# Loading the first two groups' records on SyncE behind later scatters, and one more routing step per chunk

## Chip, cores and metric

The kernel runs on one NeuronCore of a Trainium2 chip. The metric is the device time of one execution in microseconds; lower is better. Engines are written as in the profile: PE (TensorE), DVE (VectorE), ACT (ScalarE), POOL (GpSimd) and SP (SyncE, which here only issues DMAs).

## What is computed

A pooled attention (8 batches, 8 heads, 576 queries, head size 64, keys and values averaged over 8 positions to 72) is followed by a mixture of 8 experts, of which each of the 4608 tokens takes two, chosen by noisy logits. Cut to what matters:

```
k_p = k.reshape(B, H, Sp, pool, D).mean(axis=3)
v_p = v.reshape(B, H, Sp, pool, D).mean(axis=3)
attn = softmax(scale * q @ k_p^T);  x = attn @ v_p      # x: 4608 x 512
noisy_logits = x @ w_gate + log1p(exp(x @ w_noise)) * noise
top2 = the two largest of 8;  top2_w = softmax over the two
out[mask] += top2_w * (relu(x[mask] @ w1[e]) @ w2[e])   # w1: 512 x 1024, w2: 1024 x 512
```

## The kernel before

**Attention and routing.** The 36 chunks of 128 tokens are worked through in four pairs of batches (pair 0 to 3, nine chunks each). PE transposes queries (qp), multiplies them with pooled keys (s), transposes the exponentials (ep) and multiplies with pooled values (a, with the operand vbd that DVE makes from vr); DVE divides and writes the chunk (xr_b_i, batch b), and SP writes two chunks at a time to x_dram from four buffers. When a pair's logits are complete, its routing (`route`, a generator) runs in steps between the instructions of the next pair's chunks: `advance(n, m)` runs n steps of the oldest routing and then issues up to m items of the queue `scq`. Each chunk calls it with n = STEPS[pr] = 2 at one place (`adv`), and with n = 0 at up to two others (L932). Pair 3 has no next pair: its routing runs during the first stage 1 of the experts.

A routing first picks the top two on DVE and makes a mask mb. Ten small matmuls rk (L606) count the tokens per expert with mb as their operand; DVE then makes positions (pos) and records (rec, four words per token and choice). All of a pair's records are written to rec_dram, sorted by expert, by 18 scatters (L650) on POOL, each 128 rows. Between two indirect DMAs `spaced` puts a spacer, a memset of 128x512 (L501).

**Experts.** Expert 0's tokens are taken in three groups: token tiles 0 to 3, tiles 4 and 5, tiles 6 to 9. `load_recs` loads the records of a group's tiles (raw, L691). `fetch` issues a `gather` (L718) per tile, an indirect DMA on POOL from x_dram into xg. PE transposes xg (L768), stage 1 (L1030) multiplies with w1, ACT and DVE make the two parts of the hidden blocks (hh, hl; eight blocks f), and stage 2 (L1141) multiplies with w2. At the end of a tile DVE makes pv and POOL writes it to slot_dram (L1082). The load and the gathers for tiles 0 to 3 stand on POOL behind pair 1's scatters, since these tiles hold only tokens of pairs 0 and 1; those for tiles 4 and 5 stand behind pair 2's, the gathers for tiles 6 to 9 behind pair 3's. The third load of expert 0's records is issued by SP, the first two by POOL.

Each expert's weights come in eight pieces of 512 KB, loaded by SP into three buffers (wst, L459). ACT casts each piece (L480) and DVE takes the difference (L481). wst_3_1 is an expert's last piece. Each engine, and SP's queue of DMAs, works in the order in which the program issues instructions to it, and a waiting instruction holds those behind it.

Of the kernel before, what the change touches and what calls it, by code (L numbers as in the profile page):

```python
# [19 lines left out]
def kernel(  # L20
# [12 lines left out]
    nc = tc.nc  # L33
# [12 lines left out]
    NP = B // 2  # L46
    NCH = 9
# [81 lines left out]
    QS = 2  # L129
    WU = 16  # L130
    H0 = 80
    RE = 1
    PT = dict(zip(('kT', 'vTp', 'vr'), [{'o': 'one', 's': 's'}[c] for c in 'ooo']))
    EV = 0
    XE = 0
# [4 lines left out]
    STEPS = (2, 2, 2, 2)  # L140
# [350 lines left out]
    scq = []  # L491
    pace = [None]
    tail_ind = [None]
    spacer = [ap_.tile([P, DM], F32, name="spacer")]

    def spaced(make):
        if tail_ind[0] is None:
            tail_ind[0] = make()
        else:
            with tc.issue_after(tail_ind[0].ins):  # L500
                gap = nc.gpsimd.memset(spacer[0], 0.0)  # L501
            with tc.issue_after(gap.ins):
                tail_ind[0] = make()
        return tail_ind[0]

    def route(pr, c0, c1, lg, psum):
        n = c1 - c0
        k_ = [0]
# [140 lines left out]
        def scatter(c, i):  # L649
            s = spaced(lambda: nc.gpsimd.indirect_dma_start(  # L650
                out=rec_dram[:, :],
                out_offset=bass.IndirectOffsetOnAxis(ap=pos[:, i, c:c + 1], axis=0),
                in_=rec[:, c, i, :], in_offset=None))
            tc.declare_no_dep(s.ins, group="rec_scatter", reason="distinct rows")
            if pr >= NP // 2:
                tc.declare_no_dep(s.ins, group="rec_load0", reason="rows of the other half")
            if pr == NP - 1:
                tc.declare_no_dep(s.ins, group="rec_load1", reason="rows of the other pairs")
            tc.add_to_no_dep_group("rec_scatter", s.ins)
            tc.add_manual_dep(s.ins, pace[0].ins.name,  # L660
                              mybir.DependencyInfo(mybir.DependencyClass.Sync, mybir.DependencyReason.DATA),
                              reason="paced")

        for c in range(n):
            for i in range(2):
                scq.append(lambda c=c, i=i: scatter(c, i))
        if pr == NP // 2 - 1:
            scq.append(lambda: load_recs(0, 1, 0, 1, 1))
            scq.append(lambda: fetch(groups[0]))
        if pr == NP - 2:  # L670
            scq.append(lambda: load_recs(0, 1, 1, 2, 2))
            scq.append(lambda: fetch(groups[1]))
        if pr == NP - 1:
            scq.append(lambda: load_recs(0, 1, 2, 4))
            scq.append(lambda: fetch(groups[2]))
# [2 lines left out]
    def load_recs(e0, e1, s0, s1, early=0):  # L678
        ne = e1 - e0
        sect = SECT if e0 else SECT0  # L680
        t0, t1 = sect[s0][0], sect[s1 - 1][0] + sect[s1 - 1][1]
        nt = t1 - t0
        nm = f"{e0}_{t0}"
        V = nc.vector
        raw = rp.tile([P, ne, nt, RW], I32, name=f"raw{nm}")
        if s1 == len(SECT):
            V.memset(raw[64:, :, nt - 1, :], 0)
        src = rec_dram.rearrange("(e r) c -> e (r c)", e=E)
        for ts, n, np_ in sect[s0:s1]:
            o = ts * P * RW  # L690
            ld = (nc.gpsimd if RE >> (0 if early else 1 if e0 == 0 else 2) & 1 else nc.sync).dma_start(raw[:np_, :, ts - t0:ts - t0 + n].rearrange("p e t c -> p e (t c)"),  # L691
                                   src[e0:e1, o:o + np_ * n * RW].rearrange("e (p x) -> p e x", p=np_))
            if early:
                tc.add_to_no_dep_group(f"rec_load{early - 1}", ld.ins)

        for e in range(e0, e1):
            for t in range(t0, t1):
                i = (e - e0, t - t0)
                xi[e, t] = raw[:, i[0], i[1], 0:1]
                tokc[e, t] = raw[:, i[0], i[1], 2:3]  # L700
                mate[e, t] = raw[:, i[0], i[1], 3:4]
                wcol[e, t] = raw.bitcast(F32)[:, i[0], i[1], 1:2]
# [12 lines left out]
    def gather(e, t):  # L715
        xg = wp.tile([P, DM], F32, tag="xg", name=f"xg{e}_{t}", bufs=4)
        if e == 0:
            g = spaced(lambda: nc.gpsimd.indirect_dma_start(  # L718
                out=xg, out_offset=None, in_=x_dram[:XT0 if t < 4 else NTOK, :],
                in_offset=bass.IndirectOffsetOnAxis(ap=xi[e, t], axis=0)))  # L720
            if t < 4:
                tc.declare_no_dep(g.ins, group="xw1", reason="rows of the other half")
                tc.add_to_no_dep_group("xg0", g.ins)
        else:
            nr = 2 if t == 9 else 4
            row = pools[0].tile([P, DM], F32, tag="row", name=f"row{e}_{t}", bufs=4)
            turn_of("pool", lambda: nc.gpsimd.indirect_dma_start(  # L727
                out=row[:32 * nr], out_offset=None, in_=x_dram[:, :],
                in_offset=bass.IndirectOffsetOnAxis(ap=xi[e, t][:32 * nr], axis=0)))
            via = dp.tile([P, DM], F32, tag="via", name=f"via{e}_{t}", bufs=4)  # L730
            for r in range(nr):
                turn_of("sp", lambda: nc.sync.dma_start(
                    via.rearrange("(u j) (r c) -> j r u c", u=4, r=4)[:, r],
                    row[32 * r:32 * r + 32].rearrange("j (u c) -> j u c", u=4)))
            back.append(lambda: turn_of("sp", lambda: nc.sync.dma_start(xg[:, :nr * P], via[:, :nr * P])))
        XG[e, t] = xg
# [7 lines left out]
    def fetch(g):  # L744
        e, t0, nt = g
        for t in range(t0, t0 + nt):
            gather(e, t)
        while back:
            back.pop(0)()
# [44 lines left out]
    def advance(n, m):  # L794
        for _ in range(n):
            while gens:
                try:
                    next(gens[0])
                    break
                except StopIteration:  # L800
                    gens.pop(0)
        for _ in range(min(m, len(scq))):
            scq.pop(0)()
# [38 lines left out]
    for b in range(1, B):  # L842
        c = 9 * (b // 2) + (0 if b % 2 == 0 else 4)
# [44 lines left out]
    for i, (ui, u, jj) in enumerate(chunks):  # L888
        pr, ci = divmod(i, NCH)
        if ci == 0:  # L890
            lgs[pr] = (rp if pr % 2 else ap_).tile([P, NCH, H, 2 * E], F32, tag="lg", name=f"lg{pr}")
        single = u[0] == "R"
        has = ui + 1 < NU
        if single:
            order = OR
        else:
            order = OD[jj]
        eT = None
        quiet = 0 if ci == 0 and pr <= NP // 2 or ci == NCH - 1 and pr < NP // 2 else 1

        def bgs():
            for f in bg.get(i, ()):
                f()

        def adv():
            pace[0] = lastx[0]
            advance(STEPS[pr], 2 * quiet if pr >= NP // 2 else quiet)

        for o in order + ("" if "b" in order else "b") + ("" if "x" in order else "x"):
            if o == "v" and i == 0:  # L910
                drain(pg[0])
            if o == "b":
                bgs()
            elif o == "x":
                adv()
            elif o == "e":
                eT = et(u, jj)
            elif o == "v":
                if due:
                    due.pop()()  # L920
                if ci == NCH - 1 and pr < NP - 1:
                    gens.append(route(pr, 0, NCH, lgs[pr], one))
                elif ci == NCH - 1:
                    rt = route(pr, 0, NCH, lgs[pr], lambda nm: mone(nm))
                    next(rt)
                due.append(lambda u=u, jj=jj, ci=ci, eT=eT, lg=lgs[pr]: av(u, jj, ci, eT, lg))
            elif o in "012":
                if has:
                    qk(units[ui + 1], int(o))
                    if pr and (o == "0" or not single):  # L930
                        pace[0] = lasta[0]
                        advance(0, quiet)  # L932
            elif ui + 2 < NU:
                qtr(units[ui + 2], "qr".index(o))
        if i == 24:
            for _ in range(WS):
                wload()
        if i == 33:
            splits = rows_of(groups[0], one)
        if pr == 3 and ci:  # L940
            with tc.issue_after(lastl[0].ins), tc.issue_after(lasta[0].ins):
                next(first[0], None) if ci < 5 else next(first[1], None)
        if ci == 4 and pr >= HS:
            gens.append(route(pr, 0, 5, lgs[pr], one))
# [34 lines left out]
    for i in range(3):  # L979
        t = mp.tile([P, DM], F32, name=f"pv{i}")  # L980
# [356 lines left out]
```

## Time and profile before

| | |
|---|---|
| median of three runs | 1028.24 us (1027.77 to 1030.14) |
| profiled execution | 1030.06 us, its span 1028.1 us |
| granted clock, mean | 0.983 |
| busy: PE, DVE, ACT, POOL | 994.1, 551.6, 345.0, 415.1 us |
| stage 1 and 2 of the first group | from 185.21 us on |
| stage 1 of the second and third group | from 236.64 and 272.58 us on |

The span is the time from the first to the last instruction. PE is busy for 97% of it; the rest lies in a few places that the timeline shows, most of them before 280 us. A row of a timeline gives start, duration, engine, line, operation, number of instructions and, in brackets, the idle time of the engine before it with what ended that. In a row of a chain of waits stand start, duration, and what the chain runs through there.

### The profile page before, as it was taken

How to read it: one execution, taken by the hardware profiler on the slowest of the kernel's cores; microseconds unless marked ns; L12 is line 12 of the kernel's file. 1: busy time of each engine (PE TensorE's matmuls, PEld its weight loads, DVE VectorE, ACT ScalarE, POOL GpSimd, SP SyncE). 2: the span in 40 equal slices, each digit the busy share in tenths (PEclk: the TensorE clock that was granted, in tenths of full speed). 3: DMA queues.
4: the chain of work that ended last, by engine and by line, in shares of the span. 5: the costliest groups of instructions: out<-in, count | busy, mean ns of one | idle time of the engine just before them, and what ended most of it. 6: DMA issues, size and time to landing. Idle time of an engine off the chain costs nothing.

```text
span 1028.1 us, 16525 instructions
## 1 busy us (share of the span) xinstructions
PE 994.1 (97%) x5832; PEld 890.1 (87%) x5832; DVE 551.6 (54%) x1283; ACT 345.0 (34%) x857; POOL 415.1 (40%) x494
## 2 busy tenths in 40 slices
PE   7999999988899999999999999999999999999996
PEld 6798998867798988898988898989888988898995
DVE  5699988932245454644454446344544455456341
ACT  4687788521113222421232124212321232123120
POOL 4023878968500442155215421552154215422514
PEclk9899999989899999999999999999999999999999
DMA  9986954441707765676267746772677357744623
GB/s 279 341 272 222 321 187 129 142 134 27 222 35 212 205 183 148 192 245 193 76 175 242 216 125 209 243 212 74 184 241 232 114 170 245 244 145 135 210 88 135
DMA packets 137382, 190.36 MB, mean 185 GB/s; under 512 B 29155, under 2 KB 84084, under 8 KB 137274
## 3 DMA queue, kind: packets, MB, share of 16 engines
q1 hardware_dynamic: 111834, 121.84, 39.3%
q0 software_dynamic: 25440, 67.05, 21.2%
q8 instruction: 72, 1.18, 0.5%
q14 instruction: 36, 0.29, 0.1%
HBM read 126.07 MB, written 70.74 MB: 191 GB/s over the span
## 4 chain that ended last, share of the span: by engine, by line
PE 79%; DMA 6%; DVE 5%; POOL 4%; issue 3%; ACT 2%; SPq 1%; POOLq 0%; DVEq 0%; ACTq 0%
PE bank L1030 32%; PE bank L1141 23%; PE bank L1107 10%; PE a L408 5%; PE s L375 3%; PE ep L393 2%; DMA wst<-in_moe_w_dram 2%; PE qp L347 1%; POOL rec_dram L650 1%; DVE w L481 1%; POOL lg L501 1%; DMA v<-in_v_dram 1%; ACT ex L382 1%; POOL out_dram L1086 1%; DMA tab_dram<-tab 1%
## 5 line engine op out<-in xcount | busy, mean ns | idle before, releaser
L1030 PE MATMUL bank<-xh,w 128*128 128x512 f32 (+6 forms) x1536 | 390.6, 338 | 2.1 <-DVE pv L1080 1.5
L1030 PEld LDWEIGHTS bank<-xh,w 128*128 128x128 f32 x1536 | 270.3, 188 | 22.9 <-DVE pv L1080 1.7
L1141 PE MATMUL bank<-w,hh 128*128 128x512 f32 x880 | 273.9, 393 | 0.0
L1030 PE MATMUL bank<-xl,w 128*128 128x512 f32 (+6 forms) x768 | 259.7, 338 | 0.0
L1041 ACT ACTIVATE hh<-bank 128x512 fp32r<-128x512 f32 (+4 forms) x192 | 97.5, 510 | 468.7 <-PE bank L1030 444.6
L1042 DVE SCALAR_TENSOR_TENSOR hl<-bank,hh 128x512 fp32r<-128x512 f32 (+4 forms) x192 | 110.9, 579 | 241.1 <-ACT hh L1041 241.1
L1141 PEld LDWEIGHTS bank<-w,hh 128*128 128x128 f32 x880 | 166.7, 190 | 34.4
L1141 PE MATMUL bank<-w,hl 128*128 128x512 f32 x440 | 172.4, 392 | 0.0
L1030 PEld LDWEIGHTS bank<-xl,w 128*128 128x128 f32 x768 | 144.6, 188 | 10.3
L1082 POOL DMA_DIRECT2D slot_dram<-yt x17 | 9.8, 574 | 266.2 <-DVE yt L1078 218.5
L1078 DVE SCALAR_TENSOR_TENSOR pv<-bank,raw,pv 128x128 f32<-128x128 f32 x196 | 55.5, 343 | 107.0 <-PE bank L1141 58.0
L1107 PE MATMUL bank<-hh,w 128*128 128x240 f32 (+3 forms) x512 | 104.7, 300 | 2.0 <-issue 2.0
L1141 PEld LDWEIGHTS bank<-w,hl 128*128 128x128 f32 x440 | 83.3, 189 | 17.5
L1062 POOL DMA_INDIRECT pv<-slot_dram,raw x70 | 68.6, 980 | 67.9 <-DMA slot_dram<-ys 35.0
L650 POOL DMA_INDIRECT rec_dram<-rec,pos x72 | 81.1, 1127 | 36.7 <-DVE rd L415 24.5
L481 DVE TENSOR_TENSOR w<-wst,w 128x512 fp32r<-128x512 f32 x128 | 82.5, 683 | 10.4 <-ACT w L480 10.4
L1107 PEld LDWEIGHTS bank<-hh,w 128*128 128x128 f32 x512 | 83.9, 192 | 2.2 <-issue 2.2
L727 POOL DMA_INDIRECT row<-x_dram,raw x70 | 71.1, 1016 | 24.7 <-issue 20.0
L480 ACT CAST w<-wst 128x512 fp32r<-128x512 f32 x128 | 72.9, 619 | 22.7 <-DMA wst<-in_moe_w_dram 22.6
L1082 POOL DMA_DIRECT2D slot_dram<-pv x55 | 31.7, 576 | 117.4 <-DVE pv L1078 93.7
L1107 PE MATMUL bank<-hl,w 128*128 128x320 f32 (+3 forms) x256 | 76.5, 299 | 0.0
L382 ACT ACTIVATE ex<-s,mx 128x72 f32<-128x72 f32 x288 | 70.5, 345 | 8.0 <-DVE mx L380 7.8
(167 smaller groups left out, 1073.0 us busy)
## 6 DMA issues: line engine op xcount, KB each, us to landing
wst<-in_moe_w_dram SPq DMA_DIRECT2D x64, 512.0 KB
via<-row SPq DMA_DIRECT2D x266, 64.0 KB
xg<-via SPq DMA_DIRECT2D x63, 256.0 KB
slot_dram<-pv POOLq DMA_DIRECT2D x55, 256.0 KB
k<-in_k_dram SPq DMA_DIRECT2D x7, 1280.0 KB
v<-in_v_dram SPq DMA_DIRECT2D x16, 512.0 KB
x_dram<-xr SPq DMA_DIRECT2D x16, 512.0 KB
q<-in_q_dram SPq DMA_DIRECT2D x7, 1024.0 KB
```

Of the source, the lines that this page charges most:

```text
L382: lasta[0] = nc.scalar.activation(ex[:, jj, EPOS[h] * G:(EPOS[h] + 1) * G], sv[:, i], AF.Exp, bias=mx[:, i:i + 1])
L480: nc.scalar.copy(hv, sv)
L481: nc.vector.tensor_sub(lv, sv, hv.bitcast(F32))
L650: s = spaced(lambda: nc.gpsimd.indirect_dma_start(out=rec_dram[:, :], out_offset=bass.IndirectOffsetOnAxis(ap=pos[:, i, c:c + 1], axis=0), ...
L727: turn_of("pool", lambda: nc.gpsimd.indirect_dma_start(out=row[:32 * nr], out_offset=None, in_=x_dram[:, :], in_offset=bass.IndirectOffset ...
L1030: nc.tensor.matmul(part(ph), w1s(e, a, db, f), part(xs[b][:, db]), start=(i == 0), stop=(i == 3 * NDB - 1))
L1041: act = nc.scalar.activation(hh[:, :n], ph[:, :n], AF.Relu)
L1042: last = nc.vector.scalar_tensor_tensor(hl[:, :n], ph[:, :n], 0.0, hh[:, :n].bitcast(F32), op0=OP.max, op1=OP.subtract)
L1062: turn_of("pool", lambda: nc.gpsimd.indirect_dma_start(out=pv[:np_], out_offset=None, in_=slot_dram[:P + e * CAP, :], in_offset=bass.Indir ...
L1078: nc.vector.scalar_tensor_tensor(r_, y_, wc, pv[:plain] if plain else r_, op0=OP.mult, op1=OP.add)
L1107: nc.tensor.matmul(part(py), w2s(e, b, f)[:, mb * P:(mb + 1) * P], part(hs[f][a]), start=(i == 0), stop=(i == 3 * NFB - 1))
L1141: mm = nc.tensor.matmul(py, hs[f][a][:, cs], w2s(e, b, f), start=(i == 0), stop=(i == 3 * NFB - 1))
```

## The change

1. The knob RE goes. The load of records for tiles 0 to 3 and that for tiles 4 and 5 of expert 0 are issued by SP instead of POOL; that for tiles 6 to 9 is issued by POOL instead of SP.
2. The four gathers of the first group move from ahead of pair 2's scatters to behind the first two of them. The two of the second group move from ahead of pair 3's scatters to behind the first six.
3. Gathers for tiles from 4 on use `queued`: ordered behind the last indirect DMA, without a spacer.
4. Scatters may be issued at all of a chunk's places (the variable `quiet` goes), and one of these places now also runs a routing step, so that a chunk behind the first of its pair takes three steps instead of two.

```diff
-    RE = 1
@@ behind spaced
+    def queued(make):
+        with tc.issue_after(tail_ind[0].ins):
+            tail_ind[0] = make()
+        return tail_ind[0]
@@ route
         for c in range(n):
             for i in range(2):
                 scq.append(lambda c=c, i=i: scatter(c, i))
+            if pr == NP - 2 and c == 0:
+                scq.append(lambda: fetch(groups[0]))
+            if pr == NP - 1 and c == 2:
+                scq.append(lambda: fetch(groups[1]))
         if pr == NP // 2 - 1:
             scq.append(lambda: load_recs(0, 1, 0, 1, 1))
-            scq.append(lambda: fetch(groups[0]))
         if pr == NP - 2:
             scq.append(lambda: load_recs(0, 1, 1, 2, 2))
-            scq.append(lambda: fetch(groups[1]))
@@ load_recs
-            ld = (nc.gpsimd if RE >> (0 if early else 1 if e0 == 0 else 2) & 1 else nc.sync).dma_start(
+            ld = (nc.gpsimd if e0 == 0 and not early else nc.sync).dma_start(
@@ gather
-            g = spaced(lambda: nc.gpsimd.indirect_dma_start(
+            g = (spaced if t < 4 else queued)(lambda: nc.gpsimd.indirect_dma_start(
@@ the loop over chunks
-        quiet = 0 if ci == 0 and pr <= NP // 2 or ci == NCH - 1 and pr < NP // 2 else 1
-            advance(STEPS[pr], 2 * quiet if pr >= NP // 2 else quiet)
+            advance(STEPS[pr], 2 if pr >= NP // 2 else 1)
-                        advance(0, quiet)
+                        advance(o in "02" and ci > 0, 1)
```

PE, in pair 2's chunks, around the counting matmuls rk of pair 1. In a name as a_4_1_1 the numbers are the batch, its unit of two chunks, and the chunk in it. Before:

```order
L393 MATMUL ep_4_1_1_4_1749<-ident,ex_4_1_0_1489 112x128 x2
L408 MATMUL a_4_1_0_1753<-vbd_166,eT_4_1_0_1678 128x81
L375 MATMUL s_5_0_0_1824<-kbd_164,qT_5_0_1702 128x144
L347 MATMUL qp_5_0_1_1766<-ident,q_1305 128x128 x4
L325 MATMUL vr_1772<-wrb,vT_1724 112x64 x2
L325 MATMUL vr_1772<-wrb,vT_1724 112x32
L375 MATMUL s_5_0_0_1824<-kbd_164,qT_5_0_1702 128x144 x2
L375 MATMUL s_5_0_1_1849<-kbd_164,qT_5_0_1702 128x144 x3
L408 MATMUL a_4_1_1_1861<-vbd_166,eT_4_1_1_1742 128x162 x4
L408 MATMUL a_4_1_1_1861<-vbd_166,eT_4_1_1_1742 128x81 x2
L606 LDWEIGHTS before
L606 MATMUL rk_0_1779<-mb_0_1639,before 128x80
```

After, PE at the same place, up to the first rk:

```order
L346 MATMUL qp_5_0_0_1714<-ident,q_1309 128x128 x4
L316 MATMUL vTp_1729<-ident,vs_1558 128x112 x3
L407 MATMUL a_4_1_0_1799<-vbd_166,eT_4_1_0_1689 128x162 x4
L407 MATMUL a_4_1_0_1799<-vbd_166,eT_4_1_0_1689 128x81 x2
L374 MATMUL s_5_0_0_1830<-kbd_164,qT_5_0_1713 128x144 x3
L374 MATMUL s_5_0_1_1855<-kbd_164,qT_5_0_1713 128x144
L610 LDWEIGHTS before
L610 MATMUL rk_0_1742<-mb_0_1621,before 128x80
```

The first rk follows s_5_0_1's first matmul now. From the last of the ten on PE has:

```order
L610 MATMUL rk_0_1742<-mb_0_1621,ones 128x8
L392 MATMUL ep_4_1_1_0_1789<-ident,ex_4_1_0_1497 112x128 x4
L392 MATMUL ep_4_1_1_4_1795<-ident,ex_4_1_0_1497 112x128 x2
L346 MATMUL qp_5_0_1_1812<-ident,q_1309 128x128 x4
L324 MATMUL vr_1818<-wrb,vT_1733 112x64 x2
L324 MATMUL vr_1818<-wrb,vT_1733 112x32
L407 MATMUL a_4_1_1_1867<-vbd_166,eT_4_1_1_1788 128x162 x2
L392 MATMUL ep_4_2_0_0_1845<-ident,ex_4_2_0_1664 112x128 x4
```

The matmuls rk have moved ahead of ep_4_1_1, qp_5_0_1, vr, most of s_5_0_1 and a_4_1_1. Their mask mb stands on DVE fourteen instructions behind the first half of xr_4_1 in both kernels.

SP, around the last chunk's write and the last weight piece of expert 0, wst_3_1. Before:

```order
L429 DMA x_dram<-xr_7_0_0_2682 128x1024
L459 DMA wst_2_1_2735<-in_moe_w_dram 128x2x512
L459 DMA wst_3_0_2929<-in_moe_w_dram 128x2x512
L429 DMA x_dram<-xr_7_1_0_2760 128x1024
L459 DMA wst_3_1_2958<-in_moe_w_dram 128x2x512
L459 DMA wst_0_0_3027<-in_moe_w_dram 128x1024
L459 DMA wst_0_1_3055<-in_moe_w_dram 128x1024
```

After:

```order
L428 DMA x_dram<-xr_7_0_0_2686 128x1024
L458 DMA wst_2_1_2739<-in_moe_w_dram 128x2x512
L458 DMA wst_3_0_2923<-in_moe_w_dram 128x2x512
L428 DMA x_dram<-xr_7_1_0_2764 128x1024
L697 DMA raw_4_2847<-rec_dram 128x8
L458 DMA wst_3_1_2952<-in_moe_w_dram 128x2x512
L458 DMA wst_0_0_3021<-in_moe_w_dram 128x1024
```

The load raw_4, the records of tiles 4 and 5, stands directly ahead of wst_3_1 and of all pieces behind it; before, it was not in this queue.

DVE after the change, at the end of pair 3's records (rec, last operation L651), in the first group's stage 1:

```order
L647 TENSOR_TENSOR rt_0_25_2993<-rt_0_22_2983 128x9 x2
L648 SCALAR_TENSOR_TENSOR rec_0_2903<-rt_0_24_2990,rt_0_25_2993 128x9 x2
L1046 SCALAR_TENSOR_TENSOR hl_0_5_3046<-bank_2814,hh_0_5_3045 128x512
L650 TENSOR_SCALAR rt_0_25_2993<-rt_0_25_2993 128x18
L480 TENSOR_TENSOR w_3_3020<-wst_3_1_2952,w_3_3020 128x4x4x32
L651 TENSOR_TENSOR rec_0_2903<-rt_0_25_2993,tok_107 128x2x9
L480 TENSOR_TENSOR w_3_3020<-wst_3_1_2952,w_3_3020 128x4x4x32
L480 TENSOR_TENSOR w_0_3276<-wst_0_0_3021,w_0_3276 128x512 x2
L1046 SCALAR_TENSOR_TENSOR hl_0_6_3076<-bank_2815,hh_0_6_3075 128x512
L480 TENSOR_TENSOR w_0_3276<-wst_0_1_3049,w_0_3276 128x512 x2
```

The kernel before has these operations in the same order: the last operation on pair 3's records stands between the two halves of wst_3_1's subtraction.

## Rows read from the trace of the kernel before

**Rows 1.** Windows view: stretch; each engine's busy us (instructions); granted clock; DMA share; GB/s.
```profile
core 0: us, PE busy (x) PEld busy (x) DVE busy (x) ACT busy (x) POOL busy (x), PEclk, DMA share, GB/s
88.00:100.00 12.00, 10.92 (x85) 9.42 (x85) 10.42 (x31) 10.29 (x38) 7.72 (x8) 1.00 0.50 151
100.00:152.00 52.00, 52.00 (x454) 48.73 (x453) 47.35 (x144) 43.26 (x151) 41.69 (x48) 1.00 0.84 255
220.00:240.00 20.00, 18.11 (x85) 15.31 (x86) 2.93 (x7) 1.84 (x4) 18.01 (x25) 0.83 0.09 25
300.00:360.00 60.00, 60.00 (x289) 52.49 (x288) 29.40 (x71) 15.00 (x28) 14.29 (x17) 1.00 0.65 188
```

**Rows 2.** PE's timeline around the first three groups' transposes; columns as headed.
```profile
start us, us, engine line op out<-in xcount [idle before <-releaser]
...
183.19 0.72 PE L768 MATMUL xp<-ident,xg 128*128 128x128 f32 x4 [0.38 <-DMA xg<-x_dram,raw]
...
221.36 1.13 PE L768 MATMUL bank<-ident,xg 128*128 128x128 f32 x4 [2.81 <-DMA xg<-x_dram,raw]
...
223.81 1.20 PE L1141 MATMUL bank<-w,hh 128*128 128x512 f32 x2
...
227.78 0.63 PE L1141 MATMUL bank<-w,hh 128*128 128x512 f32 x2
...
248.39 0.39 PE L1030 MATMUL bank<-xh,w 128*128 128x256 f32 x1 [1.52 <-DVE pv L1080]
...
259.26 1.13 PE L768 MATMUL bank<-ident,xg 128*128 128x128 f32 x4 [3.71 <-DMA xg<-x_dram,raw]
...
265.53 1.20 PE L1141 MATMUL bank<-w,hh 128*128 128x512 f32 x2
```

**Rows 3.** POOL's timeline, loads of raw, gathers and scatters of pairs 2 and 3.
```profile
168.17 0.59 POOL L691 DMA_DIRECT2D raw<-rec_dram  x1 [0.87 <-DMA rec_dram<-rec,pos]
...
177.30 1.27 POOL L650 DMA_INDIRECT rec_dram<-rec,pos  x1 [0.17 <-issue]
...
213.69 0.58 POOL L691 DMA_DIRECT2D raw<-rec_dram  x1 [2.89 <-DMA rec_dram<-rec,pos]
217.97 1.01 POOL L718 DMA_INDIRECT xg<-x_dram,raw  x1 [3.70 <-DMA wst<-in_moe_w_dram]
...
221.35 1.02 POOL L650 DMA_INDIRECT rec_dram<-rec,pos  x1 [0.17 <-issue]
...
250.58 0.98 POOL L650 DMA_INDIRECT rec_dram<-rec,pos  x1 [0.16 <-issue]
```

**Rows 4.** DVE's timeline: masks of pairs 0 and 1, a chunk's xr, pair 2's records.
```profile
82.50 0.22 DVE L579 TENSOR_TENSOR mb<-rt,rt 128x72 bf16<-128x72 f32 x1
...
125.11 0.23 DVE L579 TENSOR_TENSOR mb<-rt,rt 128x72 bf16<-128x72 f32 x1
...
167.81 0.69 DVE L419 TENSOR_TENSOR xr<-a,rd 128x512 f32<-128x512 f32 x1
...
171.63 0.19 DVE L647 TENSOR_TENSOR rec<-rt,tok 128x18 int32<-128x18 f32 x1
```

**Rows 5.** Chain of waits, 100 to 275 us: start, us, engine, tile, line, instructions.
```profile
102.98 0.66 PE ep L393 x6
...
121.75 0.44 PE qp L347 x4
122.19 0.52 PE vr L325 x6
122.71 1.31 PE s L375 x10
124.02 1.51 PE a L408 x12
```

**Rows 6.** PE's timeline, first counting matmul of pairs 0 and 1.
```profile
83.41 0.20 PE L606 MATMUL rk<-mb,before 128*128 128x80 bf16 x1
...
125.39 0.21 PE L606 MATMUL rk<-mb,before 128*128 128x80 bf16 x1
```

**Rows 7.** Chain of waits, 300 to 400 us: a piece of weights landing.
```profile
316.43 4.41 DMA wst<-in_moe_w_dram
```

**Rows 8.** Profile page, costliest groups: busy us, mean ns of one | idle before.
```profile
L480 ACT CAST w<-wst 128x512 fp32r<-128x512 f32 x128 | 72.9, 619 | 22.7 <-DMA wst<-in_moe_w_dram 22.6
```

More of the change, by code (lines that the diff above doesn't have):

```diff
@@ L690, in load_recs @@
             o = ts * P * RW
-            ld = (nc.gpsimd if RE >> (0 if early else 1 if e0 == 0 else 2) & 1 else nc.sync).dma_start(raw[:np_, :, ts - t0:ts - t0 + n].rearrange("p e t c -> p e (t c)"),
+            ld = (nc.gpsimd if e0 == 0 and not early else nc.sync).dma_start(raw[:np_, :, ts - t0:ts - t0 + n].rearrange("p e t c -> p e (t c)"),
                                    src[e0:e1, o:o + np_ * n * RW].rearrange("e (p x) -> p e x", p=np_))
```

## The prediction

> **What bounds the kernel now.** I read the windows first, for the stretches in which TensorE (PE) has gaps; then PE's timeline, for what each gap waits for; then GpSimd (POOL) backwards from those waits. [rows 1] show PE without a gap over 100 to 152 us (52.00 of 52.00) and over 300 to 360 us, and gaps between, with a granted clock of 0.83 in 220 to 240. From 300 on the time is PE work that the change doesn't touch, so its effect must stand in PE's position when the third group's transposes are done. What PE waits for is the landing of gathers, at 221.36 (2.81 ahead of the second group's first transpose) and from 259.26 on (3.71, third group), and at 248.39 it waits 1.52 for VectorE (DVE), whose operand hangs on a slot write that POOL issues [rows 2]. Behind a gap the engine is slow too: two matmuls of L1141 take 1.20 us at 223.81 and .63 at 227.78 [rows 2], where the window's clock is 0.83, a mixture of the two levels, 1.2 and 2.4 GHz [rows 1].
>
> What makes those gathers late is one chain on POOL [rows 3]: pair 1's scatters, the load of raw at 168.17, four gathers, pair 2's 18 scatters from 177.30, raw at 213.69, two gathers from 217.97, pair 3's 18 from 221.35 to 250.58. One scatter with its spacer takes (250.58 - 221.35 - .6 for a slot write in between, as long as raw's issue at 168.17) / 17 = 1.68 us. So the place to cost the change is this chain, and whatever it newly waits for.
>
> **What the change takes off the chain.** Pair 2's first scatter no longer stands behind raw and four gathers. Its records are finished by the last DVE operation at 171.63; in the new order it stands ahead of the second half of xr_6_1, which runs at 167.81 [rows 4]. The first scatter could so start at 168.0 instead of 177.30, if attention ran as fast as now. POOL's waits ahead of the two loads (.87 and 2.89) and behind the second (3.70) go over to SyncE or vanish [rows 3]. The spacers in front of six gathers go: .7 us each, about 4 us, worth something only in the last group. The second group's gathers move behind six scatters of pair 3: 6 x 1.68 = 10.1 us that those two now stand behind, but the last group's four gain as much.
>
> **What the extra routing step costs on PE.** The step also moves the counting matmuls (rk) of pairs 0 to 2 up on PE, but not the mask mb that they read: DVE has it at the same place. For pair 1 PE used to do, ahead of rk, work that now stands behind: ep .66, qp .44, vr .52, four of ten s rows of 1.31 = .52, a 1.51 [rows 5], together 3.65 us. There mb ended at 125.34 and rk began at 125.39 [rows 4, 6]: the margin was .05. DVE now does a sum over 640 columns of k ahead of mb that stood behind it, and one vbd less; at .69 for 512 columns [rows 4] that is about .6 more. PE's stall is 3.65 - .05 + .6 = 4.2 us. Pair 0: 8 of the 12 rows of a are not among the moved, so 2.65; margin 83.41 - 82.72 = .69 [rows 4, 6]; 1280 columns of k more on DVE, 1.7: 3.7 us. Pair 2, priced by pair 1's rows: 3.65 - .05, and about 1.7 less on DVE: 1.9 us. In all 9.8. What covers this? PE has 1.08 us of gaps in 88 to 100 [rows 1] for pair 0's, and none from 100 to 152. Yet DVE is busy 47.35 of 52 there and ends of PE work are modelled, so part can be caught up: lower bound 0, upper 9.8. I take 6.5, two thirds, because the margin of .05 says that rk was already waiting for its mask and PE's order is fixed. Pair 2's first scatter then starts at 168.0 + 6.5 = 174.5.
>
> **What SyncE's wait costs.** In the old order POOL waited for a load's records; now SP's queue does. The first such load stands between two chunk writes; four xr buffers and the weights' lead hide it, and without this cover each us would delay chunk 7 by one. The second, raw_4, stands directly ahead of wst_3_1, the last weight piece of expert 0, and ahead of the next expert's pieces. The chain is worked out so. From 174.5: 2 scatters, 4 gathers, 16 scatters: 21 x 1.68 + .97, end at 210.8. From a scatter's end to the load's issue it took .87 + .54 = 1.4 us at pair 1 and 2.89 + .55 = 3.4 at pair 2 (the wait ahead of the load and one more spacer, 1.68 - .97 - .17 = .54, before it) [rows 3]; I take the middle, 2.4: raw_4 issues at 213.2, wst_3_1 .4 later at 213.6. A piece of 512 KB on a free queue landed in 4.41 us [rows 7]; with six more right behind I take 5.0: 218.6. The cast takes .62 [rows 8], the subtraction I price like it, and pair 3's last record operation stands between the two halves of that subtraction on DVE: pair 3's first scatter at 220.1, against 221.35 now. So what pair 2 won is spent at this piece.
>
> The Trainium skill, "DMA: Bandwidth & Descriptors", section "Anatomy of one DMA — SWDGE (gpsimd) path", says that a semaphore wait is done by the issuing sequencer ahead of dispatch, which speaks against a waiting load in front of unrelated weights; its fit of 2.0 us plus bytes at 436 GB/s gives an estimate of 3.2 us for the piece. The trace's 4.41 disagrees [rows 7]; by the page's figure the sum below would be 1.8 us lower.
>
> **Sum at PE.** The second group's gathers follow six scatters: 220.1 + 10.1 = 230.2. From its first gather at 217.97 to L1141 at 223.81 it takes 5.8 us now [rows 2, 3]; without the spacer of .7 it is 5.1: PE takes up L1141 again at 235.3, not 223.81: +11.5. The same piece also holds the two last hidden blocks of group 0 until about 224, which lies inside that wait. Against this stands what PE no longer waits for afterwards: 1.52 at the slot write, and from 259.26 - 3.71 = 255.55 to 265.53 [rows 2] 10.0, less 16 transposes at full clock (at most 4 x .72 by the row at 183.19; taken as 2.2, since such rows overlap) = 7.8, and of the slow matmuls behind it an estimate of 1.5 (half of the 4.0 us from 223.81 to 227.78 is excess, 1.20 against .63, and this stretch looks shorter): 10.8. Pair 3's scatters now end at about 253, its raw on POOL lands at about 259.5, the four gathers without spacers are out at 263.5 and land by 267, when PE is there (267.6). Net +11.5 - 10.8 = +0.7 us.
>
> The profiled execution took 1030.06 us, 1.8 over the median of three, 1028.24. The sum's difference is put on the median: **1028.24 + 0.7 = 1029.0**.
>
> **The rivals.** Everything hangs on t, the start of pair 2's first scatter: the result is 0.7 + (t - 174.5), as each later step moves along with t.
>
> B, faster: the masks come in time, since DVE's share has room enough or what PE loses is caught up, t is 168.0, and the difference 0.7 - 6.5 = -5.8: 1022.4. For it: DVE is 9% idle in that stretch [rows 1]. Against it: the margin of .05.
>
> C, slower: PE stalls at all three masks and nothing is caught up. Place: rk of pairs 0, 1, 2; price 9.8; t = 177.8, and +4.0: 1032.2. With DVE waiting for the stalled PE and a landing of 5.5 for the piece it reaches 1034. It decides from t = 175.9 on, a stall of 7.9 us, where the difference passes 2.1. For it: 52.00 of 52.00 busy [rows 1]. Against: busy ends are modelled.
>
> D, the wait on SP reaches nobody: the change does then not what I hold against it, pair 3's records are ready ahead, its first scatter follows pair 2's last at about 212.5, 7.6 us earlier than in my sum, and the difference is 0.7 - 7.6 = -6.9: 1021.3. Against it: the order on SP and DVE is fixed, and a piece that issues only behind raw_4 can't be cast before it lands.
>
> **How the numbers follow.** About 0.2% (2.1 us) is what a measurement here can tell from no change. Forecast A (t from 171.7 to 177, +0.7 with its own range of -2 to +3): .38, of which .30 is within 0.2%, .06 slower, .02 faster. B .24, of which .23 is faster, .01 within. C .31, of which .27 is slower, .04 within. D .07, faster. Faster .02 + .23 + .07 = .32; same .30 + .01 + .04 = .35; slower .06 + .27 = .33. The cases of both signs hold over half, so the likeliest one's own range, 1026 to 1032, stands beside the full range: from D and B's lower end, 1021, to C's upper end, 1034.
>
> **What would show it.** Right: PE waits of 2 to 4 us ahead of rk for mb in each of the first three pairs; pair 2's first scatter at 174 to 175; on SP raw_4 at about 213 with wst_3_1 right behind; casts of wst_3_1 ending near 219; one long wait of PE from about 216 to 233 and nearly none in 250 to 270. Wrong: no wait at rk (B); pair 2's first scatter after 176 (C); pair 3's records finished before wst_3_1 is cast, or this piece issued near 200 us (D). The prediction would also fail if group 0's own gathers held PE for long: the last of the four is issued at t + 8.4 = 182.9 rather than at 177.30 - 1.67 = 175.6 [rows 3], 7.3 later, where PE comes 6.5 later and already waited .38 for it [rows 2]. I cost that 1 us at nothing, as it lies ahead of PE's long wait for the second group; without that cover it adds its 1 us.

## The result

The changed kernel is **slower**: 1035.41 us in the median of 8 runs (1032.96 to 1038.82) against 1029.84 for the kernel before in the same comparison (8 runs), a ratio of 1.0057 with a 95% interval of 1.0040 to 1.0074, so 5.6 us. The forecast of +0.7 was wrong, and the time lies 1.4 us above the range's upper end; rival C had the place and the direction. The profiled execution took 1038.82 us, the slowest of the eight: it carries 6.4 us from the stretch up to 280 us, and some 2 us more from behind it, where short waits of PE at 606 and 920 us cost it 1.6 and 1.9 and the kernel before loses 2.3 at 398 us that it doesn't. The runs of some kernels below fall into two groups 5 to 6 us apart (the experiment e1: five at 1023.4 to 1026.3 us, seven at 1029.2 to 1031.6), so a difference between two such medians is known to some 3 us only.

How to count positions in what follows: loading the inputs takes a different time in each execution. DVE's xr of the twelfth chunk, just ahead of the first rk, stood at 80.61 us before, 80.89 after, and between 76.5 and 83.2 in the experiments. "Counted from the twelfth chunk" means with that time subtracted, and lateness means against the kernel before, counted so. In the four kernels that run the extra step during pair 1's chunks (the changed one, e4, f1 and g3) this chunk comes 2.25 us behind the eleventh instead of 2.80, so that lateness counted so is about .5 us too high there. Stage 1 of the third group stood at 272.58 before (191.97 counted) and stands at 279.22 after (198.33): 6.4 us late. The rows for the twelfth chunk (before, then after) and, after, for the chunk whose row at 167.81 stands in [rows 4], and for the start of that stage 1:

```profile
80.61 0.68 DVE L419 TENSOR_TENSOR xr<-a,rd 128x512 f32<-128x512 f32 x1
80.89 0.68 DVE L418 TENSOR_TENSOR xr<-a,rd 128x512 f32<-128x512 f32 x1
178.98 0.68 DVE L418 TENSOR_TENSOR xr<-a,rd 128x512 f32<-128x512 f32 x1
279.22 0.33 PE L1034 MATMUL bank<-xh,w 128*128 128x372 f32 x1
```

PE's timeline after, rows with a wait ahead; the first two answer to [rows 6], the third stands ahead of pair 2's rk, the last answers to 221.36 in [rows 2]:

```profile
85.02 0.21 PE L610 MATMUL rk<-mb,before 128*128 128x80 bf16 x1 [3.63 <-DVE mb L583]
...
131.24 0.21 PE L610 MATMUL rk<-mb,before 128*128 128x80 bf16 x1 [2.63 <-DVE mb L583]
...
171.91 0.51 PE L374 MATMUL s<-kbd,qT 128*128 128x144 f32 x2 [0.86 <-DVE rt L573]
...
226.07 0.73 PE L1145 MATMUL bank<-w,hh 128*128 128x512 f32 x2 [2.01 <-ACT hh L1045]
...
240.18 1.98 PE L774 MATMUL bank<-ident,xg 128*128 128x128 f32 x8 [3.84 <-DMA xg<-x_dram,raw]
```

At rk of pairs 0 and 1 PE stands for the mask that DVE hasn't made; before, it never waited there. The granted clock, in windows of 4 us and the stretches of [rows 1]:

```profile
84.00:88.00 4.00, 2.90 (x23) 2.21 (x23) 3.91 (x21) 1.77 (x7) 0.00 (x0) 0.71 0.84 300
88.00:92.00 4.00, 4.00 (x19) 3.95 (x19) 3.42 (x13) 1.82 (x6) 1.70 (x1) 0.50 0.04 16
92.00:96.00 4.00, 4.00 (x33) 3.48 (x33) 2.78 (x7) 1.89 (x6) 3.66 (x5) 0.94 0.03 5
128.00:132.00 4.00, 1.30 (x17) 0.97 (x16) 4.00 (x18) 0.26 (x2) 0.00 (x0) 1.00 1.02 358
132.00:136.00 4.00, 3.73 (x31) 3.35 (x30) 3.90 (x12) 3.60 (x11) 0.00 (x0) 1.00 0.79 274
100.00:152.00 52.00, 48.99 (x418) 43.85 (x417) 45.85 (x134) 41.46 (x143) 33.41 (x40) 1.00 0.73 228
220.00:240.00 20.00, 13.58 (x48) 9.58 (x47) 9.73 (x21) 6.58 (x12) 13.42 (x17) 0.90 0.77 233
260.00:280.00 20.00, 20.00 (x124) 18.07 (x123) 7.35 (x21) 3.96 (x9) 10.60 (x13) 1.00 0.71 186
```

The column ahead of the last two is the granted clock. Behind the first wait it is 0.50, the lower of the two levels (1.2 GHz): PE is busy all of 88 to 92 us, but has 19 matmuls there and 33 in the next 4 us. Behind the second wait it is 1.00. The third group's stretch, 260 to 280, has no gap any more, as forecast.

POOL's timeline, the rows that answer to [rows 3]:

```profile
179.35 0.98 POOL L654 DMA_INDIRECT rec_dram<-rec,pos  x1 [6.43 <-DVE rec L651]
...
216.23 0.98 POOL L654 DMA_INDIRECT rec_dram<-rec,pos  x1 [0.17 <-issue]
...
224.81 1.16 POOL L654 DMA_INDIRECT rec_dram<-rec,pos  x1 [5.67 <-DVE rec L651]
...
235.24 0.99 POOL L724 DMA_INDIRECT xg<-x_dram,raw  x1 [0.30 <-issue]
```

Pair 2's first scatter is not earlier than before (177.30) but 2 us later, and POOL idles 6.43 us ahead of it. Ahead of pair 3's it idles 5.67 more. What holds pair 3's records is on SP and DVE:

```profile
199.06 0.34 SPq L428 DMA_DIRECT2D x_dram<-xr  x1
218.38 0.34 SPq L697 DMA_DIRECT2D raw<-rec_dram  x1
218.84 16.25 SPq L458 DMA_DIRECT2D wst<-in_moe_w_dram  x8
```

```profile
215.85 0.25 DVE L650 TENSOR_SCALAR rt<-rt 128x18 f32<-128x18 f32 x1
223.74 0.69 DVE L480 TENSOR_TENSOR w<-wst,w 128x512 fp32r<-128x512 f32 x1 [7.65 <-ACT w L479]
224.35 0.18 DVE L651 TENSOR_TENSOR rec<-rt,tok 128x18 int32<-128x18 f32 x1
```

SP is silent from 199.4 to 218.38, where the load waits for the last scatter; the weight piece goes out behind it, and DVE, one operation short of the records at 216.1, waits 7.65 us for that piece's cast.

### The profile page after: what moved, and what is told of

Same layout as the page of the kernel before. It is cut to its first block, busy times and chain, and to the rows that moved or that the text cites. A ratio compares the mean times of both kernels' runs of the same rounds, so it can differ in the third digit from the quotient of the medians.

```text
span 1037.0 us, 16521 instructions
## 1 busy us (share of the span) xinstructions
PE 997.9 (96%) x5832; PEld 890.8 (86%) x5832; DVE 553.9 (53%) x1283; ACT 345.7 (33%) x857; POOL 411.7 (40%) x488
## 5 line engine op out<-in xcount | busy, mean ns | idle before, releaser
L1145 PE MATMUL bank<-w,hh 128*128 128x512 f32 x880 | 274.3, 393 | 2.1 <-ACT hh L1045 2.0
L1145 PEld LDWEIGHTS bank<-w,hh 128*128 128x128 f32 x880 | 166.5, 190 | 37.2 <-ACT hh L1045 2.9
L1145 PE MATMUL bank<-w,hl 128*128 128x512 f32 x440 | 172.9, 393 | 0.6 <-DVE hl L1046 0.6
L1034 PEld LDWEIGHTS bank<-xl,w 128*128 128x128 f32 x768 | 144.6, 188 | 10.8 <-issue 0.5
L654 POOL DMA_INDIRECT rec_dram<-rec,pos x72 | 79.0, 1097 | 55.1 <-DVE rec L651 42.5
L1145 PEld LDWEIGHTS bank<-w,hl 128*128 128x128 f32 x440 | 83.4, 190 | 19.0 <-DVE hl L1046 1.5
L733 POOL DMA_INDIRECT row<-x_dram,raw x70 | 73.5, 1050 | 23.7 <-issue 21.1
```

Source lines behind the costliest of these rows:

```text
L654: s = spaced(lambda: nc.gpsimd.indirect_dma_start(out=rec_dram[:, :], out_offset=bass.IndirectOffsetOnAxis(ap=pos[:, i, c:c + 1], axis=0), ...
L733: turn_of("pool", lambda: nc.gpsimd.indirect_dma_start(out=row[:32 * nr], out_offset=None, in_=x_dram[:, :], in_offset=bass.IndirectOffset ...
L1034: nc.tensor.matmul(part(ph), w1s(e, a, db, f), part(xs[b][:, db]), start=(i == 0), stop=(i == 3 * NDB - 1))
L1145: mm = nc.tensor.matmul(py, hs[f][a][:, cs], w2s(e, b, f), start=(i == 0), stop=(i == 3 * NFB - 1))
```

## Experiments

Two theories were put up. R: the loss is PE's stall at rk and the lower clock behind it, both from the extra routing step. S: the loss is SP's wait for raw_4 in front of wst_3_1. Each kernel was timed in 5 rounds beside the kernel before.

**The two halves apart.** One kernel has the loads and gathers of the change without the extra step, the other the step without the rest:

```diff
 e1_two_steps (from the changed kernel)
-                        advance(o in "02" and ci > 0, 1)
+                        advance(0, 1)
 e4_step_alone (from the kernel before)
-                        advance(0, quiet)
+                        advance(o in "02" and ci > 0, quiet)
```

> The changed kernel with the extra routing step undone (two steps per chunk again, so rk stands on PE where it stood before); loads on SyncE and moved gathers stay. Theory R (the loss is PE's stall at rk and the lower clock behind it): no PE wait at rk, the last chunk's write back at 186 us, pair 2's first scatter at about 172 instead of 179.35, and 1.5 to 3 us faster than the kernel before. Theory S (the loss is SyncE's wait for raw_4 ahead of wst_3_1): still 4 to 6 us slower than before.

> The kernel before with the extra routing step alone; loads and gathers as before. Theory R: PE waits of about 3.6, 2.6 and 1 us at rk of pairs 0, 1 and 2, granted clock of 0.5 to 0.7 behind the first, last chunk's xr about 11 us late, pair 1's last scatter near 171.4 instead of 165.8, and 5 to 6 us slower than before. Theory S: within 1 us of before, since every wait of SyncE is as before.

e1: 1029.78 us, ratio to before 0.9981 (0.9956 to 1.0006), no difference that can be told, with the sign and size that theory R gave. rk doesn't wait, and pair 2's first scatter stands at 174.87, 91.64 counted, 6.8 earlier than in the changed kernel. e4: 1037.80 us, ratio 1.0081 (1.0053 to 1.0110), a loss of 8.3 us, more than I expected and more than the whole change's. Its windows behind pair 1's rk, which waited 2.69 us:

```profile
128.00:132.00 4.00, 2.73 (x20) 2.32 (x21) 3.76 (x12) 1.29 (x4) 2.05 (x3) 0.56 1.01 273
132.00:136.00 4.00, 4.00 (x23) 3.95 (x22) 1.91 (x8) 1.95 (x7) 0.00 (x0) 0.58 0.45 150
```

The same wait as in the changed kernel (2.63), but the clock fell. So theory R holds for the loss against before, with the clock's part read from traces and not tried by itself; -1.9 and +8.3 add to +6.4, near the whole change's 5.6. But e1 with its whole chain 5 us earlier gains hardly anything, so something else eats that: its lead of 5 us at pair 2's first scatter is 2.5 at pair 3's and .5 at the third group.

**Which pair's step.** The step during one pair's chunks only:

```diff
-                        advance(o in "02" and ci > 0, 1)
+                        advance(pr == 1 and o in "02" and ci > 0, 1)   # f1: pair 0's routing
+                        advance(pr == 2 and o in "02" and ci > 0, 1)   # f2: pair 1's
+                        advance(pr == 3 and o in "02" and ci > 0, 1)   # f3: pair 2's
```

> The changed kernel with the extra routing step only during pair 1's chunks, which is pair 0's routing; rk of pairs 1 and 2 stand about where they stood before. Theory: the first stall (3.6 us) and the lower granted clock behind it cost about as much again, so attention is 5 to 6 us late from pair 1's end on and the kernel is 4 to 5 us slower than e1_two_steps, 2 to 4 us slower than before. Rival: only the stall itself counts and the clock is made up for by later slack: 2 us slower than e1_two_steps, as before.

> The changed kernel with the extra routing step only during pair 2's chunks, which is pair 1's routing. PE waits 2 to 4 us at rk of pair 1 and nowhere else; where the clock stays at 1.00 behind it attention is 3 to 4 us late, where it falls to 0.5 about 6 to 7 us late. Pair 2's first scatter is as much later than in e1_two_steps, and the kernel 3 to 6 us slower than e1_two_steps. If only pair 0's step costs: as e1_two_steps.

> The changed kernel with the extra routing step only during pair 3's chunks, which is pair 2's routing, where DVE has its mask early. Theory: PE waits 1 to 2 us there at an undisturbed clock, pair 2's records come one chunk (4 us) earlier, so pair 2's first scatter is 2 to 3 us earlier than in e1_two_steps and the kernel 2 to 3 us faster than e1_two_steps, 3 to 5 us faster than before. Rival: the step costs 4 us and more wherever it stands (stall and clock): no faster than e1_two_steps.

| kernel | wait at its rk | lowest clock behind (4 us windows) | lateness of the next xr, and some nine chunks on | ratio to before |
|---|---|---|---|---|
| f1, pair 0 | 3.64 | 0.50 | 7.0, 4.8 (6.4 by the 34th chunk) | 1.0057 (1.0039 to 1.0074) |
| f2, pair 1 | 4.65 | 0.50 | 9.5, 7.6 | 1.0064 (1.0044 to 1.0084) |
| f3, pair 2 | 4.39 | 0.50 | 6.2, 6.5 (three on) | 0.9957 (0.9941 to 0.9973) |

Each of f1 and f2 alone costs as much as all three together, and some 8 us against e1 (0.9981), more than the 4 to 5 and 3 to 6 that I expected. A wait of 3.6 to 4.7 us leaves attention 6 to 8 us late at its end (the 34th chunk: 6.4, 8.1 and 6.5). In f3 PE waits more than I expected (4.39, not 1 to 2: rk stands right behind s there too, ahead of ep, qp, vr and a), yet the kernel gains, since pair 2's records come earlier by more than attention is late: its first scatter starts at 167.27, 89.70 counted, 1.9 earlier than in e1. So the step costs where it stalls PE and pays only for the pair whose records the chain waits for. The price of the clock shows where the wait at pair 1 is equal: from the twentieth to the 31st chunk the changed kernel (2.63, clock 1.00) fell back by 4.6 us, g3 below, the same program up to there, (2.64, 0.60) by 6.2, and e4 (2.69, 0.56) by 7.2.

**SyncE's wait.** Theory S again, now for what e1 didn't gain. In e8 the load of raw_4 is issued four scatters of pair 3 later, which puts it on SP behind wst_3_1 and five more pieces; e5 has it on GpSimd instead; g3 is e8's edit on the changed kernel, step and all:

```diff
 e8_raw_behind_weights (from e1), g3_after_raw_behind (from the changed kernel)
-        if pr == NP - 2:
-            scq.append(lambda: load_recs(0, 1, 1, 2, 2))
+            if pr == NP - 1 and c == 1:
+                scq.append(lambda: load_recs(0, 1, 1, 2, 2))
 e5_raw_on_pool (from e1)
-            ld = (nc.gpsimd if e0 == 0 and not early else nc.sync).dma_start(
+            ld = (nc.gpsimd if e0 == 0 and early != 1 else nc.sync).dma_start(
```

> e1_two_steps with the load of raw_4 put into the queue four scatters of pair 3 later, which places it on SyncE behind wst_3_1 and the next expert's first five pieces. Theory S, and theory R as far as e1 keeps a wait there: wst_3_1 issues at about 200 us, pair 3's first scatter follows pair 2's last at about 211 instead of 218 in e1, second group's gathers at about 221: 4 to 7 us faster than before. If SyncE's wait reaches nobody: as e1, within 1 us.

> e1_two_steps with the load of raw_4 back on GpSimd, directly behind pair 2's last scatter; the two gathers stay behind six scatters of pair 3. GpSimd waits 2 to 3 us there for the scatter to land, pair 3's first scatter at about 214, gathers at about 224, so 1 to 3 us slower than e8 and 2 to 5 us faster than before by theory S. If SyncE's wait reaches nobody: 2 to 3 us slower than e1.

> The changed kernel, step and all, with only the load of raw_4 put behind wst_3_1 and the next expert's first five pieces on SyncE. If stall and SyncE's wait are separate costs that add: PE's waits at rk stay (3.6, 2.6, about 1 us), pair 3's first scatter follows pair 2's last at about 218 instead of 225, and the kernel is 4 to 6 us faster than the changed one, within 2 us of before. If the late attention alone sets the end: within 1.5 us of the changed kernel.

e8: 1022.28 us, ratio 0.9930 (0.9907 to 0.9952). e5: 1022.73, 0.9938 (0.9915 to 0.9961). g3: 1030.62, 1.0024 (1.0005 to 1.0044), some 3.4 us under the changed kernel by the two ratios, a little less than expected, and 2.5 over the kernel before. POOL in e8:

```profile
170.97 0.97 POOL L654 DMA_INDIRECT rec_dram<-rec,pos  x1 [4.59 <-DVE rec L651]
...
210.47 1.16 POOL L654 DMA_INDIRECT rec_dram<-rec,pos  x1 [0.84 <-DVE rec L651]
...
222.90 0.98 POOL L724 DMA_INDIRECT xg<-x_dram,raw  x1 [2.53 <-DMA raw<-rec_dram]
```

Pair 3's first scatter follows pair 2's last with .84 us of idling, where the changed kernel idled 5.67 and e1 7.36. Whether the load then stands on SP or on POOL makes no difference that the ratios can tell (I had expected 1 to 3 us; in the traces e5's third group stands 1.0 us behind e8's). That it no longer stands ahead of the weight piece is worth 5 us without the step (e8 against e1) and 3.4 with it, each known to some 3 us. In g3 pair 3's first scatter came 1.9 us earlier than in the changed kernel (142.04 counted against 143.92), not 7 as expected, and the third group .7 earlier. But the clock fell there behind the second wait, and its first group started 3.1 us later (119.69 against 116.61), so 3.8 us were won between the two places. Theory S is right too: both costs are there, and the changed kernel lost the one and missed the other.

**The step where it pays, on top.** e9 is e8 with f3's line.

> e8_raw_behind_weights with the extra step during pair 3's chunks only. By the first theory of f3_step_pair2 the whole chain of GpSimd starts 2 to 3 us earlier than in e8 and this kernel is 1 to 3 us faster than e8, about 1020 us. By its rival: 2 us slower than e8.

1023.41 us, ratio 0.9958 (0.9940 to 0.9976), not faster than e8: the expectation missed. The chain is 1.9 us earlier there, but the third group stands at 186.87 counted against e8's 186.98: PE, 6 us late in attention, gives it back (argued from the trace; by the ratios, whose intervals overlap, the two can't be told apart).

**The first group's gathers.** In e1, e5 and e8 PE waits for the first gather. Its timeline in e1:

```profile
185.35 0.72 PE L774 MATMUL xp<-ident,xg 128*128 128x128 f32 x4 [4.28 <-DMA xg<-x_dram,raw]
186.91 1.10 PE L774 MATMUL xp<-ident,xg 128*128 128x128 f32 x4 [0.84 <-DMA xg<-x_dram,raw]
```

That gather was issued at 178.22, and PE had it 7.1 us later. e10 is e8 with the four gathers back ahead of pair 2's scatters:

```diff
-            if pr == NP - 2 and c == 0:
-                scq.append(lambda: fetch(groups[0]))
         if pr == NP // 2 - 1:
             scq.append(lambda: load_recs(0, 1, 0, 1, 1))
+            scq.append(lambda: fetch(groups[0]))
```

> e8_raw_behind_weights with the first group's four gathers back ahead of pair 2's scatters. PE's wait for xg_0, 4.4 us in e8, is gone; pair 2's first scatter starts at about 176 to 177 instead of 171 to 172, and the chain to the third group's gathers moves along by 5 us. If that chain is the bound: 3 to 5 us slower than e8. If PE's start of the first group is the bound: 2 to 4 us faster than e8.

1017.60 us, ratio 0.9914 (0.9896 to 0.9932), the fastest of all, though 0.16% under e8 is inside the two intervals; counted from the twelfth chunk its third group is 4.5 us ahead of e8's. I had given the chain's bound the first place, and it fell. PE's longest wait for data in e10 is the one at the second group (sum, times, longest):

```profile
PE bank L773 <- DMA xg<-x_dram,raw: 5.4, 1, 5.4
```

Pair 2's first scatter is later than in e8 (174.81, 96.38 counted, against 91.64), but pair 3's is earlier (206.80, 128.37 counted, against 131.14). Most of that, 2.2 us, is there at pair 2's last scatter already (126.57 counted against 128.78): the four gathers run from 168.12 on, in the time in which POOL idled 4.59 us for pair 2's records in e8, and no longer between these scatters. The rest is the wait ahead of pair 3's: its routing runs inside the first group's stage 1, which begins 6.9 us earlier when PE doesn't wait for xg_0, and its records are ready when POOL comes. At the second group's gathers another 2.5 us come on top, since e8's wait for raw_4 there is gone.

**The second group sooner.** g1 is e10 with raw_4 on GpSimd behind pair 2's last scatter and the two gathers behind four scatters of pair 3:

```diff
-            if pr == NP - 1 and c == 1:
-                scq.append(lambda: load_recs(0, 1, 1, 2, 2))
-            if pr == NP - 1 and c == 2:
+            if pr == NP - 1 and c == 1:
                 scq.append(lambda: fetch(groups[1]))
+        if pr == NP - 2:
+            scq.append(lambda: load_recs(0, 1, 1, 2, 2))     # on GpSimd
```

> e10_gathers_ahead with the load of raw_4 on GpSimd directly behind pair 2's last scatter and the second group's two gathers behind four scatters of pair 3 instead of six. PE's wait of 5.4 us ahead of the second group falls to 2 to 4 us; pair 3's last scatter and the third group's gathers come as late as in e10 or 1 to 3 us later (GpSimd's wait for the load). If the third group's gathers are the bound by then: within 2 us of e10. If the second group's wait is the bound: 2 to 3 us faster.

1024.91 us, ratio 0.9954 (0.9940 to 0.9968): slower than e10, outside both expectations. In its profile, which is the slowest of its six runs, the load's wait (2.98 us) stands in front of all 18 scatters of pair 3; the wait at the second group didn't fall (5.64), and four waits, 3.1 us together, come back at the third. So the third group is the bound in that trace, and what the load took from POOL reached it; one trace doesn't show it for the median.

## Why the prediction was wrong, point by point

**The bound** was read rightly. In every kernel with the second group's gathers behind six scatters, the third group's stage 1 starts 42.8 to 44.8 us behind the first of these gathers, so it moved with POOL's chain and what feeds it. The spacers left out and the scatters at more places (points 3 and 4 of the change) were not tried alone. The one long wait that I gave as a sign, from 216 to 233, didn't come: PE, 12 us late from attention, was still at the first group and waited 2.0, .5 and 3.8 us between 224 and 240.

**The stall at rk is the step that failed**: the 6.5 us that I took for attention's lateness, and with it t. The waits were 3.63, 2.63 and, ahead of the third rk, .86 (at a matmul of s, not for the mask), where the working had 3.7, 4.2 and 1.9. Their sum, 7.1, is near the 6.5 by luck: only the first of the three terms held, and "two thirds" stood for work caught up, which isn't why the others were smaller. But attention came 10.9 us late (the xr at 167.81 in [rows 4] now stands at 178.98; counted from the twelfth chunk), above my upper bound of 9.8, because that sum held no clock. [rows 2] showed what a gap does to the matmuls behind it, I said so in the first paragraph, and I left it out of this sum. Behind the first wait the next xr was 7.6 us late, twice the wait. "None from 100 to 152" was right: nothing of pair 1's was caught up. And "part can be caught up" had no row in its support: only some of pair 0's was, from 7.6 to 6.3 in seven chunks, near the 1.08 us of gaps in [rows 1]. (The 21st chunk, ahead of pair 1's rk, shows 5.1, but the step itself brings it forward: in f2, with nothing late before it, it stands 1.3 us early.) From the twentieth chunk to the 31st another 4.6 us were lost. PE's windows between their xr, before and after:

```profile
118.93:167.81 48.88, 48.38 (x430) 44.21 (x428) 45.48 (x164) 39.70 (x135) 38.81 (x47) 1.00 0.60 182
125.52:178.98 53.46, 49.31 (x428) 44.12 (x426) 47.02 (x176) 41.82 (x143) 30.50 (x37) 1.00 0.49 161
```

3.6 of them are gaps (4.15 against .50), mostly the waits of 2.63 and .86; the remaining .9 at a clock of 1.00 I can't place.

**From pair 2's first scatter on the sum holds, in part by terms that cancel.** The start was at 179.35, or 179.07 with the later input taken off (178.5 counted from the eleventh chunk), instead of 174.5. From there to pair 3's first scatter I had 45.6 us; it took 45.5. The way to the end of pair 2's last scatter took 37.9 (36.3); the load's issue came 1.2 behind that (2.4 in the sum, 1.4 its lower end), wst_3_1 .46 behind it, pair 3's first scatter 6.0 behind that (6.5). Six scatters took 10.4 (10.1). From the second group's first gather to L1145 it took 6.6 (5.1), which is most of what is left. The waits behind, 10.8 us, went as forecast: from L1145 to the third group's stage 1 it took 37.4 us, before 48.8. (PE's place there, 267.6, doesn't follow from the sum's own terms, 235.3 + 255.55 - 223.81 - 1.52 = 265.5; nothing came of it, since PE waited for nothing there.) The rule of the rivals, 0.7 + (t - 174.5), gives +5.3 for t = 179.07; the profile shows +6.4 and the medians +5.6. One wrong term, carried through, made most of the error; the kernels that change only the step follow the rule to within 1.5 us, with t taken to the input time of before: f2 (180.39, rule +6.6, measured 0.64%), f1 (178.26, +4.5, 0.57%), e1 (172.25, -1.6, -0.19%), f3 (170.31, -3.5, -0.43%). The median that I added to, 1028.24, was itself 1.6 below the one of the joint comparison; on that one C's upper end would have stood at 1035.6.

**SP's wait** was read rightly, place and price, and rival D fell: DVE waited 7.65 us for that piece's cast. Without the wait, in e8, pair 3's first scatter came 7.1 us earlier than in e1 (131.14 counted against 138.22), near D's 7.6. The Trainium skill ("DMA: Bandwidth & Descriptors", "Anatomy of one DMA — SWDGE (gpsimd) path") says that any semaphore wait happens on the issuing sequencer before dispatch. The trace agrees: SP issues nothing from 199.40 to 218.38. The Trainium skill's fit there, which the prediction set beside the piece, is one for the gpsimd path, while SP issues the piece. The sum's 5.0 was near: the piece, issued at 218.84, was there for its cast at 223.09, 4.25 us later.

**The first group's gathers** I costed at nothing, 1 us if uncovered. In the changed kernel PE waits 1.02 for them, as worked out there. But the cover was attention's lateness itself: without the stall (e1) it is 4.3 us, because PE is there in time and the gathers are issued later. Their landing is no news: PE had the first one 7.1 us after its issue, and before the change the last of the four 7.6 us after (175.6 to 183.19 in [rows 2]). Whether those 4.3 us reach the end, and so whether rival B's 1022.4 left out a cost, is open: e1 came out where the rule puts it (-2.0 against -1.6), with nothing left for them, while e10, which takes them away together with POOL's idling, stands 4.5 us ahead at the third group.

## What to carry to other kernels

When an instruction is moved up on an engine that has no gaps, look whether its operand moves up too; if not, the operand's engine now sets the pace, and the price is the wait plus what the clock takes behind it. A load with a long wait must not stand in a queue ahead of transfers that others need: the same load behind the weight pieces, or on GpSimd, turned a change of -0.2% into one of -0.7 or -0.6% against the kernel before. And a gather moved off the chain that it delays must still land before its reader; here, put back, the gathers also filled time in which POOL idled.

## What the hardware showed that I had not expected

PE's granted clock went to 0.50 behind waits of 3.63 to 4.65 us, at rk in all kernels with such a wait, and the first window of 4 us at 1.00 again began 7 to 12 us after the wait's end; behind waits of 2.63 to 2.69 us there it stayed at 1.00 in the changed kernel and fell to 0.56 and 0.60 in e4 and g3. Gathers of 128 rows of 2 KB were there 7.1 us after their issue while weight pieces and chunk writes were under way (e1, issued 178.22, DMA share 0.84 until then), 4.4 us with weight pieces alone (e1, 231.75, share 0.89), and 3.4 us with a share of 0.34 (217.97 in [rows 3]); what sets the difference was not tried.
